# Separate tiles for the high and low parts of both layers' weights, one subtraction and a copied tail in the second layer, rotations that end in one sum

## The chip, the cores and the metric

The kernel runs on one core of a Trainium2 chip. The metric is the time of the whole program on the device in microseconds (us), lower being better. The engines are named as in the profile: PE (TensorE, matmuls), PEld (its weight loads), DVE (VectorE), ACT (ScalarE), POOL (GpSimd) and SP (SyncE). SP and POOL issue the transfers between the device memory and the chip's own memory (SBUF).

## The reference

One layer of a sequence model works on 2048 tokens of 576 numbers, in float32. A condition vector gives six modulation rows. The first half is a diagonal state-space convolution over the whole length, the second a feed-forward net with ReLU and 4608 hidden units:

```python
x = A_u                                            # 1 x 2048 x 576
mod = (_silu(c) @ w_mod).reshape(1, 6, 1, -1)      # sa, ca, ga, sb, cb, gb
h = _layernorm(x) * (1 + ca) + sa
# K[d, l] = 2 Re sum_n C[d, n] dt[d] exp(A[d, n] dt[d] l),  l = 0..2047
y = irfft(rfft(h, 4096) * rfft(K, 4096))[:2048] + h * D_skip
x = x + ga * y
h = _layernorm(x) * (1 + cb) + sb
x = x + gb * (relu(h @ w1) @ w2)                   # w1: 576 x 4608, w2: 4608 x 576
```

## The kernel before

**Stages.** The tokens are four blocks of 512. From the start to about 225 us the kernel computes the modulation, the powers from which the long filter K is built, and the convolution of block 0. Then the feed-forward net runs over the blocks 0 to 3, and beside it a generator of other work, a piece at a time: beside block 0 the rest of the filter (`rest`, with 12 "heads") and the convolution of block 1; beside block 1 the end of block 0, another six heads of `rest`, and the convolution of block 2; beside block 2 the end of block 1 and the convolution of block 3; beside block 3 the end of block 2.

**Two parts of each number.** TensorE multiplies in a reduced float32 format (`F32R`). To keep the accuracy, each factor is split into a high part (rounded to that format) and a low part (the rest), and a product takes three matmuls: high by high, high by low, low by high. The hidden layer is cut into 36 slices of 128 units, so that g runs from 0 to 143 over the four blocks. For each slice `first(g)` does 14 matmuls of 128x512 into the bank `hps`; ACT takes the ReLU's high part (`hh`, L1337) and DVE the low one (`hl`, L1338); `second(g-1)` does 14 more into the accumulators `acc`. On PE `first(g+1)` comes ahead of `second(g)`.

**The weights.** For each slice SP loads the raw weights of layer one (`r1`) and layer two (`r2`). ACT rounds them: `hi1` (L1297, 640 columns) and `hi2` (L1307, 576 columns). In block 0 DVE subtracts to get the low parts: `lo1` (L1302, 640 columns) and `lo2` (L1313 for the last 64 columns, L1314 for the first 512). SP then stores the low parts to device memory (`L1d`, `L2d`, L1415), and in the blocks 1 to 3 loads them back (L1286, L1317) so that DVE needn't compute them again. High and low part of a slice of layer one lie in one tile `w1`, of which there are three; those of layer two in one tile `w2` of 1152 columns, also three. A tile may be written again only when everything that read or wrote its old contents is done. So `hi1` waits, beside the matmuls, for the store of the old low part to have landed. In `w2` the last 64 high columns and the last 64 low ones lie side by side, because `second` multiplies them in one 128-column weight (into `acc4`).

**Rotations.** A head of `rest` turns complex numbers W by complex factors Z: it needs, per rotation, two multiplications of 128x1536 (T = W times the imaginary part, L482; W1r = W times the real part, L484) and two sums of 128x768 (real part minus, L486; imaginary part plus, L488). Block 0 has 24 rotations, block 1 has 12. W0 and Z (in the profile `Zr`) are loaded through POOL's queue; the load of a head's Z stands right behind that of its W0, which waits until a buffer of W0 is free. After the rotations PE forms the products `kps` in two halves (L517, 96 small matmuls each) that ACT copies out (`ker`, L527); there is one bank for them, so the second half waits until the first is copied out.

**What sets the order.** Within each engine the order is fixed before the run by a scheduler that goes by the program order, the dependences and costs of its own. The program order is set by `step(g)`, four times per slice: it draws pieces from the generator until the yielded costs (the numbers behind `yield`, in us of DVE) reach a target that grows with g, at most 2.7 per call.

Of the kernel before, what the change touches and what calls it, by code (L numbers as in the profile page):

```python
# [18 lines left out]
P = 128  # L19
# [30 lines left out]
class KGen:  # L50
# [403 lines left out]
    def rest(self, psum, plan):  # L454
# [5 lines left out]
        with ExitStack() as ctx:  # L460
# [15 lines left out]
            def rot(out, X, Z, i):  # L476
                T = pt.tile([P, 2, H, 16], F32, tag="T", name="T")
                zr, zi = (
                    Z[:, i, r].unsqueeze(1).unsqueeze(3).broadcast_to([P, 2, H, 16])
                    for r in range(2)  # L480
                )
# [4 lines left out]
                v(out[:, 0], out[:, 0], T[:, 1], op=ALU.subtract)  # L486
                yield 0.95
                v(out[:, 1], out[:, 1], T[:, 0], op=ALU.add)  # L488
# [83 lines left out]
class Body:  # L572
# [692 lines left out]
    def ffn(self, gens):  # L1265
# [17 lines left out]
        def low1(g):  # L1283
            w = w1[g] = ff.tile([P, 2, 5, P], F32R, tag="w1", bufs=3, name="w1")
            if g >= NF:
                nc.sync.dma_start(  # L1286
                    out=w[:, 1].rearrange("p k c -> p (k c)").bitcast(F32), in_=self.L1d[g % NF]
# [8 lines left out]
        def hi1(g):  # L1296
            copy(g - 1)(w1[g][:, 0], r1[g], AF.Copy)  # L1297

        def lo1(g):
            w, r = w1[g], r1.pop(g)  # L1300
            if g < NF:
                vec(g)(w[:, 1], r, w[:, 0], op=ALU.subtract)  # L1302
                late.append((self.L1d[g], w[:, 1].rearrange("p k c -> p (k c)")))

        def hi2(g):
            w = w2[g] = ff.tile([P, 1152], F32R, tag="w2", bufs=3, name="w2")
            copy(g)(w[:, 0:D], r2[g], AF.Copy)  # L1307

        def lo2(g):
            w, r = w2[g], r2.pop(g)  # L1310
            if g < NF:
                v = vec(g)
                v(w[:, D:640], r[:, 512:D], w[:, 512:D], op=ALU.subtract)  # L1313
                v(w[:, 640:], r[:, :512], w[:, :512], op=ALU.subtract)  # L1314
                late.append((self.L2d[g], w[:, D:]))
            else:
                nc.sync.dma_start(out=w[:, D:].bitcast(F32), in_=self.L2d[g % NF])  # L1317

        def first(g):
# [3 lines left out]
            ops = [(w[:, 0, 4], xs), (w[:, 1, 4], xs)]  # L1323
            if g:
                for k in range(4):
                    ops += [(w[:, 0, k], xh[:, k]), (w[:, 0, k], xl[:, k]), (w[:, 1, k], xh[:, k])]
# [237 lines left out]
```

## Time and profile before

| | |
|---|---|
| median of 3 runs | 1333.58 us (1330.17 to 1338.6) |
| the profiled execution | 1333.12 us, span 1331.4 us |
| mean granted clock of TensorE | 0.945 of full speed |
| PE busy | 1209.0 us, 91% |
| DVE busy | 895.4 us, 67% |
| ACT busy | 494.5 us, 37% |
| POOL busy | 162.8 us, 12% |

The page's times are those of one execution. Busy is the sum of an engine's instructions. The timeline prints for each instruction its start, its length, the engine, line, operation, output and inputs, and in brackets how long the engine stood idle before it and what ended that wait. The view by stretches of time prints per stretch its length, then for PE, PEld, DVE, ACT and POOL the busy time with the number of instructions, then the granted clock of TensorE, the share of the DMA engines and GB/s. The accumulators are copied out (L1443) at 549.73, 1091.73 and 1317.91 us for the blocks 0, 2 and 3, and the rotations run on DVE from 233 to 393 us (block 0) and from 572 to 643 us (block 1).

### The profile page before, as it was taken

To read this page: it belongs to the slowest core of one execution; us is meant where nothing else is said; L and a number is where in the kernel's file an instruction comes from. 1 tells how busy PE (TensorE), PEld (TensorE's weight loads), DVE (VectorE), ACT (ScalarE), POOL (GpSimd) and SP (SyncE) were. 2 spreads that over 40 slices of the span, in tenths; PEclk is the share of its full clock that TensorE was granted. 3 is DMA by queue.
4 is the path that set the end of the run, shared out by engine and by line. 5 is a ranking of instruction groups with operands and counts; after the bars stand their busy time and mean duration, and the time that the engine had idled before them with its cause. 6 is when DMAs were issued, how large, how long until landed. Compare 5 with 4: busy or idle time off the path is not lost.

```text
span 1331.4 us, 25993 instructions
## 1 busy us (share of the span) xinstructions
PE 1209.0 (91%) x10720; PEld 956.7 (72%) x10720; DVE 895.4 (67%) x1324; ACT 494.5 (37%) x863; POOL 162.8 (12%) x260
## 2 busy tenths in 40 slices
PE   4566676989989999999999999999999999999997
PEld 3344554667767687777777887887888888888885
DVE  5989988999986999689468993558995231111112
ACT  5678623222223422622243225433223453232321
POOL 0756502011000100100001000100000000000000
PEclk9557788999999999999999999999999999999999
DMA  8557982989878967799879985868996557666651
GB/s 272 214 221 296 304 307 84 350 296 331 307 253 304 337 224 277 247 402 342 281 276 338 357 321 156 288 203 305 346 363 198 175 181 223 198 198 202 192 168 54
DMA packets 122379, 345.85 MB, mean 260 GB/s; under 512 B 23916, under 2 KB 24212, under 8 KB 111508
## 3 DMA queue, kind: packets, MB, share of 16 engines
q1 hardware_dynamic: 105364, 226.96, 51.2%
q0 software_dynamic: 16384, 115.85, 23.1%
q8 instruction: 84, 1.38, 0.4%
q10 hardware_dynamic: 512, 1.38, 0.3%
q14 instruction: 35, 0.29, 0.1%
HBM read 262.73 MB, written 81.40 MB: 258 GB/s over the span
## 4 chain that ended last, share of the span: by engine, by line
PE 68%; DVE 17%; DMA 7%; issue 4%; ACT 2%; POOL 1%; SPq 0%; ACTq 0%; DVEq 0%; POOLq 0%
PE acc L1358 28%; PE hps L1332 27%; PE ps_f L852 5%; DMA L1d<-w 3%; PE kps L71 2%; PE ph L71 2%; DVE T L482 2%; DVE W1r L484 2%; PE ps_i L1059 2%; PE kps L517 1%; DVE w L1302 1%; DVE W1r L486 1%; DVE W1r L488 1%; DVE w L1314 1%; DVE T L62 1%
## 5 line engine op out<-in xcount | busy, mean ns | idle before, releaser
L1332 PE MATMUL hps<-xh,w 128*128 128x512 f32 x1152 | 395.2, 403 | 1.2 <-ACT xh L47 1.2
L1358 PE MATMUL acc<-w,hh 128*128 128x512 f32 x1152 | 366.4, 400 | 3.3 <-ACT hh L1337 3.2
L1338 DVE SCALAR_TENSOR_TENSOR hl<-hps,hh 128x512 fp32r<-128x512 f32 x144 | 99.0, 687 | 311.5 <-ACT hh L1337 310.8
L1332 PEld LDWEIGHTS hps<-xh,w 128*128 128x128 f32 x1152 | 217.8, 190 | 49.7 <-ACT xh L47 2.5
L1358 PEld LDWEIGHTS acc<-w,hh 128*128 128x128 f32 x1152 | 215.1, 188 | 50.6 <-ACT hh L1337 4.1
L1332 PE MATMUL hps<-xl,w 128*128 128x512 f32 x576 | 228.5, 397 | 0.7 <-DVE xl L47 0.5
L1358 PE MATMUL acc<-w,hl 128*128 128x512 f32 x576 | 223.1, 399 | 1.8 <-DVE hl L1338 1.8
L1337 ACT ACTIVATE hh<-hps 128x512 fp32r<-128x512 f32 x144 | 86.0, 597 | 327.7 <-PE hps L1332 320.5
L1307 ACT ACTIVATE w<-r 128x576 fp32r<-128x576 f32 x141 | 96.7, 686 | 216.5 <-PE acc L1358 216.1
L1332 PEld LDWEIGHTS hps<-xl,w 128*128 128x128 f32 x576 | 109.4, 190 | 24.7 <-DVE xl L47 1.7
L1358 PEld LDWEIGHTS acc<-w,hl 128*128 128x128 f32 x576 | 107.7, 189 | 26.1 <-DVE hl L1338 3.7
L1297 ACT ACTIVATE w<-r 128x640 fp32r<-128x640 f32 x140 | 102.6, 733 | 59.1 <-DMA L1d<-w 53.8
L1332 PE MATMUL hps<-xs,w 128*128 128x512 f32 x288 | 97.8, 409 | 0.0
L71 PE MATMUL kps<-W,W 128*32 128x16 f32 x2304 | 39.6, 210 | 47.3 <-POOL W L68 28.4
L1038 DVE TENSOR_TENSOR Y<-Y,T 128x1152 f32<-128x1152 f32 x60 | 79.3, 1349 | 0.0
L71 PEld LDWEIGHTS kps<-W,W 128*32 128x32 f32 x2304 | 34.8, 143 | 60.7 <-POOL W L68 31.0
L853 ACT ACTIVATE Z<-ps_f 128x288 f32<-128x288 f32 x120 | 49.0, 410 | 70.5 <-PE ps_f L852 68.5
L517 PEld LDWEIGHTS kps<-W1r,W2r 128*32 128x32 f32 x3456 | 45.2, 113 | 38.4 <-issue 19.7
L517 PE MATMUL kps<-W1r,W2r 128*32 128x48 f32 (+2 forms) x3456 | 52.5, 202 | 15.6 <-ACT ker L527 9.4
L1478 POOL DMA_DIRECT2D out_dram<-x x16 | 8.7, 545 | 466.9 <-DVE x L1470 464.5
L1332 PEld LDWEIGHTS hps<-xs,w 128*128 128x128 f32 x288 | 53.2, 188 | 11.1
L1358 PE MATMUL acc<-hh,w 128*128 128x512 f32 x144 | 57.5, 399 | 0.0
(235 smaller groups left out, 1574.5 us busy)
## 6 DMA issues: line engine op xcount, KB each, us to landing
r<-in_w_dram SPq DMA_DIRECT2D x144, 320.0 KB, 6.0
r<-in_w_dram SPq DMA_DIRECT2D x144, 288.0 KB, 3.9
w<-L1d SPq DMA_DIRECT2D x108, 320.0 KB, 4.1
w<-L2d SPq DMA_DIRECT2D x108, 288.0 KB, 2.8
W2r<-W2d POOLq DMA_DIRECT2D x18, 1536.0 KB, 9.4
W2d<-W SPq DMA_DIRECT2D x12, 1536.0 KB, 8.6
Ua<-Ud POOLq DMA_DIRECT2D x15, 1152.0 KB, 9.5
W<-W1d POOLq DMA_DIRECT2D x18, 768.0 KB, 9.6
```

The lines of the kernel that those rows point to most:

```text
L71: self.tc.keep_in_program_order(self.nc.tensor.matmul(*args, **kw))
L482: v(T, X, zi, op=ALU.mult)
L517: nc.tensor.matmul(ps[32 * dd : 32 * dd + 32, q, :], W2[:, r, ch], W1[:, r, ch], start=(r == 0), stop=(r == 1),)
L852: nc.tensor.matmul(o, fc[:, n2, c, :], src(n2), start=True, stop=True)
L853: ev = nc.scalar.activation(Z[:, n2, c], ps[:, :PC], AF.Copy)
L1038: v(y, y, T, op=op or ALU.add)
L1297: copy(g - 1)(w1[g][:, 0], r1[g], AF.Copy)
L1307: copy(g)(w[:, 0:D], r2[g], AF.Copy)
L1332: nc.tensor.matmul(ps, a, x, start=(i == 0), stop=(i == 13))
L1337: nc.scalar.activation(hh, ps, AF.Relu)
L1338: nc.vector.scalar_tensor_tensor(hl, ps, 0.0, hh, op0=ALU.max, op1=ALU.subtract)
L1358: nc.tensor.matmul(acc[i], a, x, start=(f == 0 and seen[i] == 1), stop=(f == NF - 1 and seen[i] == (3 if i < 4 else 2)),)
```

## The change

There are four edits.

1. Layer one: the high part lies in a tile `w1h` of its own (three of them), the low part in a tile `w1l` (four of them).
2. Layer two: the high part lies in `w2h` (640 columns, three tiles), the low part in `w2l` (576 columns, three tiles). `lo2` is one subtraction of 576 columns. The last 64 low columns must still lie beside the last 64 high ones, so ACT copies them: one new ACT instruction of 128x64 per slice (after.py L1317), in all 144 slices. In block 0 it reads what `lo2` wrote, in the blocks 1 to 3 what the load of `L2d` brought.
3. Rotations: Z has a third row, minus the imaginary part, which a new ACT instruction (L490, 128x2x48, one per head, 18 in all) makes from the loaded row; so it waits for the load. The load's rows are no longer contiguous in the tile. T then holds W times (imaginary, minus imaginary), and one sum of 128x1536 with T's halves swapped (L485) ends the rotation.
4. At a block's end the tile t4 is taken from a shared tile.

```diff
-                Z = pt.tile([P, 2, 2, H], F32, tag="Z", bufs=3, name=f"Zr_{h}")
+                Z = pt.tile([P, 2, 3, H], F32, tag="Z", bufs=3, name=f"Zr_{h}")
                 d(out=W0.rearrange("p r c a -> p (r c a)"), in_=k.W1d[h])
-                d(out=Z.rearrange("p i r c -> p (i r c)"), in_=k.Zd[h])
+                d(out=Z[:, :, 0:2], in_=k.Zd[h].rearrange("p (i r c) -> p i r c", i=2, r=2))
...
-                v(out[:, 0], out[:, 0], T[:, 1], op=ALU.subtract)
-                yield 0.95
-                v(out[:, 1], out[:, 1], T[:, 0], op=ALU.add)
-                yield 0.95
+                v(out, out, T[:, ::-1], op=ALU.add)
+                yield 1.75
 
             def rots(h, W1, W0, Z):
                 blocks = plan[h]
+                nc.scalar.activation(Z[:, :, 2], Z[:, :, 1], AF.Copy, scale=-1.0)
...
-            w = w1[g] = ff.tile([P, 2, 5, P], F32R, tag="w1", bufs=3, name="w1")
+            w = ff.tile([P, 5, P], F32R, tag="w1l", bufs=4, name="w1l")
+            w1[g] = [None, w]
...
-            copy(g - 1)(w1[g][:, 0], r1[g], AF.Copy)
+            w = w1[g][0] = ff.tile([P, 5, P], F32R, tag="w1h", bufs=3, name="w1h")
+            copy(g - 1)(w, r1[g], AF.Copy)
...
-            w = w2[g] = ff.tile([P, 1152], F32R, tag="w2", bufs=3, name="w2")
+            w = ff.tile([P, 640], F32R, tag="w2h", bufs=3, name="w2h")
+            w2[g] = w, ff.tile([P, D], F32R, tag="w2l", bufs=3, name="w2l")
             copy(g)(w[:, 0:D], r2[g], AF.Copy)
...
-                v = vec(g)
-                v(w[:, D:640], r[:, 512:D], w[:, 512:D], op=ALU.subtract)
-                v(w[:, 640:], r[:, :512], w[:, :512], op=ALU.subtract)
-                late.append((self.L2d[g], w[:, D:]))
+                vec(g)(l, r, w[:, 0:D], op=ALU.subtract)
+                late.append((self.L2d[g], l))
             else:
-                nc.sync.dma_start(out=w[:, D:].bitcast(F32), in_=self.L2d[g % NF])
+                nc.sync.dma_start(out=l.bitcast(F32), in_=self.L2d[g % NF])
+            copy(g)(w[:, D:], l[:, 512:], AF.Copy)
```

The order on the engines moves as follows. First ACT where the rotations of block 0 end. Before (w1 and w2 are the weight tiles, r1 and r2 the raw weights, hh the hidden slices 17 and 18, ker the copies out of the products):

```order
L1337 ACTIVATE hh_5214<-hps_5186 128x512
L1297 ACTIVATE w1_5224<-r1_5002 128x640
L527 ACTIVATE ker_6_3271<-kps_5066 128x16x6
L527 ACTIVATE ker_6_3271<-kps_5123 128x16x6
L1307 ACTIVATE w2_5302<-r2_5004 128x576
L1337 ACTIVATE hh_5298<-hps_5275 128x512
```

The slice 18's `hh` is the first row here, behind the two copies of the second-last head's products. The same place now:

```order
L1338 ACTIVATE hh_5130<-hps_5059 128x512
L525 ACTIVATE ker_0_3118<-kps_4917 128x48x6
L1317 ACTIVATE w2h_4954<-w2l_4955 128x64
L525 ACTIVATE ker_0_3118<-kps_4996 128x48x6
L1308 ACTIVATE w2h_5259<-r2_4899 128x576
L1317 ACTIVATE w2h_5134<-w2l_5135 128x64
L525 ACTIVATE ker_6_3281<-kps_5073 128x16x6
L525 ACTIVATE ker_6_3281<-kps_5143 128x16x6
L1317 ACTIVATE w2h_5259<-w2l_5260 128x64
L1297 ACTIVATE w1h_5358<-r1_5053 128x640
L1338 ACTIVATE hh_5255<-hps_5226 128x512
```

The first row is the slice 17's `hh`, the last the slice 18's; between them stand both heads' copies, one `hi2`, one `hi1` and three of the new tail copies (L1317).

Next ACT at the start of block 1's rotations, from the slice 38's `hh` to the slice 40's. Before:

```order
L1337 ACTIVATE hh_6572<-hps_6557 128x512
L1297 ACTIVATE w1_6580<-r1_6483 128x640
L1307 ACTIVATE w2_6619<-r2_6485 128x576
L1337 ACTIVATE hh_6615<-hps_6600 128x512
L1297 ACTIVATE w1_6623<-r1_6553 128x640
L1307 ACTIVATE w2_6674<-r2_6555 128x576
L1337 ACTIVATE hh_6670<-hps_6655 128x512
```

And now:

```order
L1338 ACTIVATE hh_6642<-hps_6627 128x512
L490 ACTIVATE Zr_6_6607<-Zr_6_6607 128x2x48
L1308 ACTIVATE w2h_6692<-r2_6552 128x576
L1317 ACTIVATE w2h_6692<-w2l_6693 128x64
L1297 ACTIVATE w1h_6755<-r1_6623 128x640
L1338 ACTIVATE hh_6688<-hps_6673 128x512
L490 ACTIVATE Zr_7_6613<-Zr_7_6613 128x2x48
L1308 ACTIVATE w2h_6750<-r2_6625 128x576
L490 ACTIVATE Zr_8_6715<-Zr_8_6715 128x2x48
L1317 ACTIVATE w2h_6750<-w2l_6751 128x64
L1297 ACTIVATE w1h_6810<-r1_6669 128x640
L1338 ACTIVATE hh_6746<-hps_6731 128x512
```

Three of the new negations (L490, the heads 6, 7 and 8) stand between the three `hh`, each ahead of the next slice's `hh`. The next one (head 9) stands behind the slice 41's `hh` and right ahead of the first `ker` of this block:

```order
L1338 ACTIVATE hh_6801<-hps_6786 128x512
L490 ACTIVATE Zr_9_6842<-Zr_9_6842 128x2x48
L525 ACTIVATE ker_6_6814<-kps_6815 128x32x6
L1308 ACTIVATE w2h_6911<-r2_6729 128x576
L1317 ACTIVATE w2h_6911<-w2l_6912 128x64
```

On ACT the copy of the products thus comes only after this head's load.

Last DVE, within a rotation of block 0 (T and W1r as above, hl the hidden slice's low part). Before:

```order
L1338 SCALAR_TENSOR_TENSOR hl_3731<-hps_3713,hh_3730 128x512
L486 TENSOR_TENSOR W1r_2_3600<-W1r_2_3600,T_3663 128x48x16
L488 TENSOR_TENSOR W1r_2_3600<-W1r_2_3600,T_3663 128x48x16
L1313 TENSOR_TENSOR w2_3734<-r2_3447,w2_3734 128x64
L482 TENSOR_TENSOR T_3721<-W1r_2_3600,Zr_2_3238 128x1536
```

And now:

```order
L485 TENSOR_TENSOR W1r_2_3611<-W1r_2_3611,T_3676 128x96x16
L1339 SCALAR_TENSOR_TENSOR hl_3744<-hps_3727,hh_3743 128x512
L481 TENSOR_TENSOR T_3719<-W1r_2_3611,Zr_2_3245 128x1536
L1313 TENSOR_TENSOR w2l_3748<-r2_3447,w2h_3747 128x576
L1302 TENSOR_TENSOR w1l_3675<-r1_3445,w1h_3752 128x640
```

One sum (L485) stands for the two, and one subtraction (L1313, now 576 columns) for L1313 and L1314.

More of the change, by code (lines that the diff above doesn't have):

```diff
@@ L477, in rot @@
                 T = pt.tile([P, 2, H, 16], F32, tag="T", name="T")
[L478 to L481, printed above, removed]
+                cb = [P, 2, H, 16]
+                zr = Z[:, i, 0].unsqueeze(1).unsqueeze(3).broadcast_to(cb)
+                zi = Z[:, i, 1:3].unsqueeze(3).broadcast_to(cb)
                 v(T, X, zi, op=ALU.mult)
@@ L1466, in finish @@
         yield None
-        t = self.cv.tile([P, 4, 64], F32, tag="t4", bufs=1, name="t4")
+        t = self.half("t4")[:, :, 0:64]
         v(t, ps, gb[:, 512:].unsqueeze(1).broadcast_to([P, 4, 64]), op=ALU.mult)
```

21 lines of the change are left out of this document (11 added, 10 removed).

## The prediction

> **What bounds the kernel now.** I read the page's head first, then the busy times by stretch, cut at the ends of the rotations, of two stalls and of the blocks.
>
> ```profile
> span 1331.4 us, 25993 instructions
> PE 1209.0 (91%) x10720; PEld 956.7 (72%) x10720; DVE 895.4 (67%) x1324; ACT 494.5 (37%) x863; POOL 162.8 (12%) x260
> 224.80:394.00 169.20, 153.65 (x2512) 117.82 (x2512) 164.20 (x176) 44.56 (x81) 18.52 (x35) 0.98 0.84 304
> 394.00:402.40 8.40, 7.44 (x117) 5.68 (x121) 0.11 (x2) 1.99 (x6) 1.05 (x1) 0.60 0.46 184
> 402.40:510.70 108.30, 108.01 (x638) 83.49 (x638) 95.36 (x155) 36.88 (x74) 8.25 (x15) 1.00 0.82 295
> 510.70:520.50 9.80, 6.80 (x23) 4.81 (x22) 9.16 (x12) 3.10 (x5) 0.00 (x0) 0.83 0.77 306
> 520.50:549.70 29.20, 29.12 (x130) 22.95 (x128) 23.09 (x53) 14.47 (x27) 0.00 (x0) 1.00 0.72 235
> 549.70:823.00 273.30, 271.76 (x2261) 215.24 (x2260) 208.37 (x265) 99.73 (x186) 24.89 (x43) 1.00 0.85 307
> 823.00:1091.70 268.70, 268.70 (x1181) 218.16 (x1180) 166.87 (x234) 99.12 (x178) 12.37 (x22) 1.00 0.75 257
> ```
>
> In the rotations of block 0 (to 394 us) DVE is full: 164.20 of 169.20. From 402 us PE is full, and stays so through the blocks 1 and 2 (271.76 of 273.30, 268.70 of 268.70). So the blocks 1 and 2 can only lose by a change that leaves PE's work alone, as this one does. Gains are to be had in block 0: on DVE in the rotations, and in the two short stretches with clocks 0.60 and 0.83. What ends the waits there shows in the list of waits and the timelines of ACT, PE and DVE:
>
> ```profile
> ACT w L1297 <- DMA L1d<-w: 53.8, 11, 11.3
> 393.29 0.74 ACT L1297 ACTIVATE w<-r 128x640 fp32r<-128x640 f32 x1 [6.99 <-DMA L1d<-w]
> 394.50 0.41 ACT L527 ACTIVATE ker<-kps 128x288 f32<-128x288 f32 x1
> 394.96 2.17 PE L517 MATMUL kps<-W1r,W2r 128*32 128x48 f32 x96 [4.70 <-ACT ker L527]
> 402.38 0.69 DVE L1338 SCALAR_TENSOR_TENSOR hl<-hps,hh 128x512 fp32r<-128x512 f32 x1 [8.29 <-ACT hh L1337]
> 513.96 0.74 ACT L1297 ACTIVATE w<-r 128x640 fp32r<-128x640 f32 x1 [11.34 <-DMA L1d<-w]
> 515.81 0.50 PE L1358 MATMUL acc<-w,hh 128*128 128x512 f32 x1 [2.77 <-ACT hh L1337]
> ```
>
> `hi1` waits eleven times, 53.8 us together, for the store of the old low part. At 393 and 514 us this reaches PE: `hi1` holds ACT, behind it stand `ker` or `hh`, and PE stops and then runs at a lower clock. The other nine lie under DVE's rotations.
>
> **Edit 1, `hi1` without the store.** With its own tile `hi1` waits only for matmuls that are done.
>
> First stall: PE stood from 390.26 (394.96 less 4.70), 3.74 us of it ahead of 394.00. Behind that 8.40 us passed with 7.44 busy at clock 0.60, which is 7.44 x 0.60 = 4.5 at full clock. At most 3.74 + 8.40 - 4.5 = 7.6 us come back. Not quite all: the last head's products need DVE's last rotation, which ends at the first stretch's end, and `hh` now stands behind both heads' copies and three tail copies. I take 6.5, and a range of 3 to 7.6.
>
> Second stall: 9.80 - 6.80 x 0.83 = 4.2 us at most. But DVE is busy for 9.16 of these 9.80, and the low parts that PE wants come from there; I take 2, range 0 to 4.2.
>
> The store's wait moves to `lo1` on DVE, where `w1l` has four tiles instead of three: one slice later. A slice is at least the 6.35 us from one `hh` to the next (580.28 to 586.62 below), so of 11.34 at most 5.0 would be left, and of 6.99 some 0.6.
>
> **Edits 2 and 3 on DVE.** What an instruction costs on a full engine is the distance between starts, not its length:
>
> ```profile
> 344.93 0.94 DVE L486 TENSOR_TENSOR W1r<-W1r,T 128x768 f32<-128x768 f32 x1
> 345.79 0.95 DVE L488 TENSOR_TENSOR W1r<-W1r,T 128x768 f32<-128x768 f32 x1
> 346.66 0.21 DVE L1313 TENSOR_TENSOR w<-r,w 128x64 fp32r<-128x64 f32 x1
> 346.80 1.75 DVE L482 TENSOR_TENSOR T<-W,Zr 128x1536 f32<-128x1536 f32 x1
> 348.47 0.68 DVE L1314 TENSOR_TENSOR w<-r,w 128x512 fp32r<-128x512 f32 x1
> 349.07 0.81 DVE L1302 TENSOR_TENSOR w<-r,w 128x640 fp32r<-128x640 f32 x1
> 436.16 0.75 DVE L867 TENSOR_TENSOR W<-Z 128x576 f32<-128x576 f32 x1
> 436.82 0.75 DVE L873 TENSOR_TENSOR K<-W 128x576 f32<-128x576 f32 x1
> 257.86 1.76 DVE L484 TENSOR_TENSOR W1r<-W,Zr 128x1536 f32<-128x1536 f32 x1 [1.88 <-PE kps L517]
> 314.47 1.76 DVE L484 TENSOR_TENSOR W1r<-W,Zr 128x1536 f32<-128x1536 f32 x1 [1.76 <-PE kps L517]
> ```
>
> Two sums: 346.66 - 344.93 = 1.73; one 1536-element instruction: 348.47 - 346.80 = 1.67. A rotation saves 0.06, 24 rotations 1.4 us. `lo2`: 0.14 + 0.60 (346.66 to 346.80, 348.47 to 349.07) against 0.66 for 576 elements (436.16 to 436.82): 0.08, and 1.4 over the 18 slices that the rotations span. Together 2.8. By plain lengths it would be 0.94 + 0.95 - 1.75 = 0.14 and 0.21 + 0.68 - 0.75 = 0.14, so 24 x 0.14 + 18 x 0.14 = 5.9; I go by the starts, since DVE is full, and keep 5.9 as the far end.
>
> [...]
>
> DVE also waits twice for `kps`, 1.88 + 1.76 = 3.6 us, where ACT's `ker` had stood behind a waiting `hi1`; I take half, 1.8. Against that stands edit 3's negation early on: ahead of the third slice's `hi1` ACT now waits for the third head's Z, and DVE's `lo1` behind it comes late. The bounds are 0 and a Z load's landing (below); I take 1.8. The remaining negations in block 0 stand ahead of `hh`s that DVE reaches microseconds later, so I cost them at nothing; without that cover each costs what Z is late. The rotations: -2.8 - 1.8 + 1.8 = -2.8.
>
> **Edit 3 in block 1.** Here PE is full, and the negation puts a DMA wait into ACT's queue: `hi2`, `hi1`, `hh` and `ker` queue behind it, and PE behind these. The rows of before, with POOL's issues of Z:
>
> ```profile
> 573.34 0.60 ACT L1337 ACTIVATE hh<-hps 128x512 fp32r<-128x512 f32 x1 [2.49 <-PE hps L1332]
> 580.28 0.60 ACT L1337 ACTIVATE hh<-hps 128x512 fp32r<-128x512 f32 x1 [2.49 <-PE hps L1332]
> 586.62 0.60 ACT L1337 ACTIVATE hh<-hps 128x512 fp32r<-128x512 f32 x1 [2.48 <-PE hps L1332]
> 588.18 0.39 PE L1358 MATMUL acc<-w,hl 128*128 128x512 f32 x1
> 595.07 0.72 PE L517 MATMUL kps<-W1r,W2r 128*32 128x32 f32 x48
> 571.60 1.76 DVE L482 TENSOR_TENSOR T<-W,Zr 128x1536 f32<-128x1536 f32 x1 [9.63 <-DMA Zr<-Zd]
> 576.44 0.55 POOL L47 DMA_DIRECT2D Zr<-Zd  x1
> 588.03 0.54 POOL L47 DMA_DIRECT2D Zr<-Zd  x1
> DMA to landing us min/median/max: 2.3/8.5/15.9
> L527 ACT ACTIVATE ker<-kps 128x192 f32<-128x192 f32 x12 | 4.0, 337 | 5.7 <-PE kps L517 5.7
> ```
>
> Head 6: Z lands by 571.6; negation 0.3 (an estimate from `ker`, 0.34), `hi2` 0.6, tail 0.2, `hi1` 0.65 bring `hh` of slice 39 to 573.3, where it is now: free. Head 8: issued at 576.44, landing 8.5 later at 584.9; then negation, tail and `hi1` bring `hh` of slice 40 (580.28) to 586.1, and `hl` to about 587.4. PE wants that `hl` at 588.18: free, barely. Head 9: issued at 588.03, landing at 596.5, and only then `ker` of the first products, at 596.9 to 597.2; PE wants to begin their second half at 595.07 now. It stops for 2.1 us, and about 1 more goes to the clock behind a stop, as at 394 and 511 us. The heads 10 and 11 stand where PE, by then 3 us later, leaves room. I take 3; with landings of 2.3 it is 0, with 15.9 it is 595.07 to 604.6, 9.5, and some 3 for the clock.
>
> **Edit 2's tail copies.** In block 0 the copy waits for `lo2`, and stands where DVE has done it. In the blocks 1 to 3 it waits for the load of `L2d`:
>
> ```profile
> w<-L2d SPq DMA_DIRECT2D x108, 288.0 KB, 2.8
> 438.01 0.69 ACT L1307 ACTIVATE w<-r 128x576 fp32r<-128x576 f32 x1
> 438.80 0.41 ACT L853 ACTIVATE Z<-ps_f 128x288 f32<-128x288 f32 x1
> 440.05 0.41 ACT L853 ACTIVATE Z<-ps_f 128x288 f32<-128x288 f32 x1 [0.84 <-PE ps_f L852]
> ```
>
> That load can issue when the low tile's last matmul is done, about 0.7 us before `hi2` can start, so 2.8 later it has landed 2.1 behind `hi2`'s start; in the plain slices ACT waits 2.5 us for `hh` anyway, so it is covered. In the convolutions of the blocks 1 and 2 one copy of a spectrum (Z) follows `hi2`, then the tail, and the next Z is due 1.25 us after the one before: 440.05 - 438.01 = 2.0 behind `hi2`. It comes some 0.3 us late, against 0.84 that it has. I take 1.5 for about eleven such tails, range 0 to 4. Edit 4 moves one small tile: nothing.
>
> **The sum**: -6.5 - 2 - 2.8 + 3 + 1.5 = -6.8 on 1333.12, so 1326.3 for an execution like the profiled one; the median of the runs stands 0.46 above that: 1326.8, say 1327.
>
> **The rivals.** *All of the slack comes back*: the stalls whole (7.6 + 4.2), both `kps` waits (3.6), the merges by plain lengths (5.9), and no Z late: -21.3, 1312. For it: of all heads' Zs DVE waited long for one, at 571.60. Against it: DVE's 9.16 of 9.80 in the second stall. 0.25.
>
> *The store's wait only moves*, to `lo1` on DVE, which in block 0 has no room, or `hh` loses behind tail copies that wait for `lo2` what `hi1` gains: then the first stall gives 3, the second nothing, the rotations nothing, and block 1 takes its 4.5: +1.5, 1335. For it: DVE's 164.20 of 169.20. Against it: the fourth tile. 0.20.
>
> *The negation holds ACT*, on the other side: Z landing near 15.9, as it did at its worst. It decides from the point where head 9's Z lands after 595: block 1 pays 12.5, the tails 4, and in block 0 four of the twelve heads let DVE wait 3 us each, 12, against gains of 6.5 + 2 + 2.8: +17.2, 1351. For it: W0's 768 KB go ahead of each Z in the same queue. Against it: the median of 8.5. 0.13. [...]
>
> **The numbers.** The forecast has 0.42, and by its own bounds reaches from 1318 to 1335. A difference of 1%, 13 us, is about what can be told apart from no change. Faster by more takes a time under 1320: the first rival and a little of the forecast, 0.28. Slower by more, over 1347: most of the third, 0.12. Within: 0.60. The range reaches into both outer rivals, 1312 to 1345.
>
> **What would show it.** In the profile of the changed kernel: no wait of `hi1` for `L1d`, and no stretch at a clock of 0.60 about 390 us; DVE's rotations ending near 390; block 0 ending near 538 instead of 549.70, the cut in the stretches; ACT's negations waiting for Zr, and a PE wait for `ker` of 2 us about 585; the blocks 1 and 2 together longer by 4 to 5 than their 273.30 + 268.70 = 542.0 us. I am wrong if `lo1` or the tail copies show the waits that `hi1` had, if DVE waits in the rotations for negations, or if block 1 loses more than 6 us.

## The result, and the profile after

| | us |
|---|---|
| before, median of 6 runs | 1332.29 (1328.69 to 1338.60) |
| after, median of 6 runs | 1390.21 (1388.14 to 1398.36) |
| ratio after to before, 95% interval | 1.0443 (1.0412 to 1.0475) |
| profiled execution of after | 1390.04, span 1388.3 |

The changed kernel is 58 us slower. That is outside the range, and beyond even the rival on the slow side (1351). The head of its page, and the two groups of ACT and DVE that changed most:

```profile
span 1388.3 us, 26053 instructions
PE 1226.9 (88%) x10720; PEld 969.9 (70%) x10720; DVE 891.3 (64%) x1252; ACT 524.3 (38%) x1025; POOL 165.9 (12%) x260
L1339 DVE SCALAR_TENSOR_TENSOR hl<-hps,hh 128x512 fp32r<-128x512 f32 x144 | 99.4, 691 | 370.2 <-ACT hh L1338 370.0
L1317 ACT ACTIVATE w2h<-w2l 128x64 fp32r<-128x64 f32 x141 | 35.9, 254 | 274.2 <-DMA w2l<-L2d 267.0
```

ACT's new copy of the tail (line 1317) is 35.9 us of work in an engine that is idle for 62% of the span; but ACT stood still for 267.0 us ahead of it, waiting for the load of the second layer's low part.

Where the time went shows in the busy times by block, cut at the copies of `acc` out of PSUM that end each block. The columns are the stretch, its length, the busy times of PE, PEld, DVE, ACT and POOL, the granted clock, the DMA share and GB/s. First after:

```profile
224.80:553.80 329.00, 306.17 (x3423) 238.88 (x3422) 288.62 (x334) 111.86 (x244) 30.09 (x50) 0.96 0.81 290
553.80:872.90 319.10, 291.20 (x2296) 227.92 (x2295) 208.44 (x253) 107.16 (x230) 26.02 (x43) 0.97 0.77 268
872.90:1150.20 277.30, 263.29 (x1132) 212.06 (x1132) 165.24 (x231) 101.62 (x208) 12.34 (x22) 0.97 0.72 241
1150.20:1376.30 226.10, 226.10 (x1003) 187.43 (x1002) 30.57 (x46) 75.71 (x141) 2.17 (x4) 1.00 0.61 181
```

and the same cuts in the kernel before:

```profile
224.80:549.70 324.90, 305.02 (x3409) 234.75 (x3409) 291.92 (x393) 101.00 (x190) 27.83 (x50) 0.97 0.81 292
549.70:833.80 284.10, 282.56 (x2309) 224.15 (x2308) 210.08 (x267) 103.66 (x193) 24.89 (x43) 1.00 0.84 303
833.80:1091.70 257.90, 257.90 (x1133) 209.25 (x1132) 165.16 (x231) 95.19 (x172) 12.37 (x22) 1.00 0.76 259
1091.70:1317.90 226.20, 226.20 (x1003) 187.45 (x1002) 30.46 (x46) 67.60 (x108) 2.18 (x4) 1.00 0.61 182
```

Block 0 is 4 us longer where 11 were to be gained, block 1 is 35.0 longer, block 2 19.4 longer, and block 3 the same. (From block 1 some twelve matmuls have moved to block 0, as the counts show; what moves them is said with the table of the experiments.) In block 1 PE, which had no room, now stands idle for 319.1 - 291.2 = 27.9 us, and its granted clock is 0.97 where it was 1.00.

Block 3 has the tail copies too, 34 of them in this cut. ACT's waits for the load, in the lists of waits cut to the blocks 1 and 3 (us in total, times, longest):

```profile
ACT w2h L1317 <- DMA w2l<-L2d: 126.6, 31, 12.2
ACT w2h L1317 <- DMA w2l<-L2d: 53.2, 34, 3.0
```

In block 3 ACT waits 53.2 us and nothing is lost; in block 1 it waits 126.6. What differs is how long the load takes to land. It is the same 288 KB through the same queue; its median is the last number in these rows, from the DMA views of after, cut to the blocks 1, 2 and 3:

```profile
w2l<-L2d SPq DMA_DIRECT2D x36, 288.0 KB, 5.1
w2l<-L2d SPq DMA_DIRECT2D x36, 288.0 KB, 3.2
w2l<-L2d SPq DMA_DIRECT2D x34, 288.0 KB, 2.8
```

The medians alone don't tell the loss apart, since that of block 2 is close to that of block 3. The longest landings are 8.9, 7.4 and 4.3 us, and ACT's timeline has 20 waits of more than 2.5 us for the load in block 1, 11 in block 2 and one in block 3. What they have above 2.5 us adds up to 59.1, 25.4 and 0.5 us.

How a late load reaches PE is seen in one place in block 1, where the convolutions run. The timelines of SP's queue, ACT and PE of after:

```profile
738.38 0.33 SPq L1316 DMA_DIRECT2D w2l<-L2d  x1
...
739.08 0.69 ACT L1308 ACTIVATE w2h<-r 128x576 fp32r<-128x576 f32 x1 [1.21 <-PE acc L1359]
739.67 0.39 ACT L851 ACTIVATE Z<-ps_f 128x288 f32<-128x288 f32 x1
740.90 0.41 ACT L851 ACTIVATE Z<-ps_f 128x288 f32<-128x288 f32 x1 [0.84 <-PE ps_f L850]
746.37 0.26 ACT L1317 ACTIVATE w2h<-w2l 128x64 fp32r<-128x64 f32 x1 [5.05 <-DMA w2l<-L2d]
746.53 0.39 ACT L851 ACTIVATE Z<-ps_f 128x288 f32<-128x288 f32 x1
...
741.63 0.65 PE L850 MATMUL ps_f<-kt,fcK 128*128 128x288 f32 x2
742.34 0.39 PE L1333 MATMUL hps<-xh,w1h 128*128 128x512 f32 x1
...
746.98 1.33 PE L850 MATMUL ps_f<-kt,fcK 128*128 128x288 f32 x2 [4.01 <-ACT Z L851]
747.69 1.04 PE L1333 MATMUL hps<-xh,w1l 128*128 128x512 f32 x1
```

The load is issued at 738.38 and its copy starts 8.0 us later. The matmuls of the next spectrum, issued at 741.63, had taken 0.65 us, but its copy (`Z`, line 851) stands behind the tail on ACT and starts at 746.53, 0.16 us after the tail does. PE stops for 4.01 us until `Z` is copied. Behind the stop two matmuls of 288 columns take 1.33 us and one of 512 takes 1.04, where ahead of it they had taken 0.65 and 0.39. Two loads of 1152 KB each for the next convolution were issued meanwhile, at 739.30 and 739.82, and took 9.4 and 12.0 us.

### The profile page after: what moved, and what is told of

It is laid out like the page before. It is cut to its first block, busy times and chain, and to the rows that moved or that the text cites. A ratio compares the mean times of both kernels' runs of the same rounds, so it can differ in the third digit from the quotient of the medians.

```text
span 1388.3 us, 26053 instructions
## 1 busy us (share of the span) xinstructions
PE 1226.9 (88%) x10720; PEld 969.9 (70%) x10720; DVE 891.3 (64%) x1252; ACT 524.3 (38%) x1025; POOL 165.9 (12%) x260
## 4 chain that ended last, share of the span: by engine, by line
PE 61%; DVE 16%; DMA 13%; issue 6%; ACT 3%; POOL 1%; SPq 0%; ACTq 0%; POOLq 0%; DVEq 0%
PE acc L1359 24%; PE hps L1333 23%; DMA w2l<-L2d 7%; PE ps_f L850 4%; DMA Zr<-Zd 2%; PE kps L71 2%; PE ph L71 2%; PE ps_i L1057 2%; PE kps L515 2%; DVE T L1034 1%; DVE Y L1036 1%; DVE T L481 1%; DMA W<-W1d 1%; DVE W1r L485 1%; DVE W1r L483 1%
## 5 line engine op out<-in xcount | busy, mean ns | idle before, releaser
L1359 PE MATMUL acc<-w2h,hh 128*128 128x512 f32 x576 | 231.1, 406 | 9.7 <-ACT hh L1338 9.7
L1333 PE MATMUL hps<-xh,w1l 128*128 128x512 f32 x576 | 235.2, 408 | 0.0
L1333 PE MATMUL hps<-xh,w1h 128*128 128x512 f32 x576 | 233.7, 406 | 0.7 <-ACT xh L47 0.7
L1359 PE MATMUL acc<-w2l,hh 128*128 128x512 f32 x576 | 233.3, 410 | 0.0
L1333 PE MATMUL hps<-xl,w1h 128*128 128x512 f32 x576 | 229.1, 398 | 0.1
L1359 PE MATMUL acc<-w2h,hl 128*128 128x512 f32 x576 | 222.9, 400 | 2.5 <-DVE hl L1339 2.4
L1317 ACT ACTIVATE w2h<-w2l 128x64 fp32r<-128x64 f32 x141 | 35.9, 254 | 274.2 <-DMA w2l<-L2d 267.0
L1359 PEld LDWEIGHTS acc<-w2h,hh 128*128 128x128 f32 x576 | 110.6, 192 | 36.1 <-ACT hh L1338 12.3
L1333 PEld LDWEIGHTS hps<-xh,w1h 128*128 128x128 f32 x576 | 111.0, 193 | 25.3 <-ACT xh L47 1.3
L1333 PEld LDWEIGHTS hps<-xh,w1l 128*128 128x128 f32 x576 | 110.7, 192 | 24.1 <-issue 0.3
L1333 PEld LDWEIGHTS hps<-xl,w1h 128*128 128x128 f32 x576 | 110.3, 191 | 24.6 <-DVE xl L47 0.4
```

Source lines behind the costliest of these rows:

```text
L1317: copy(g)(w[:, D:], l[:, 512:], AF.Copy)
L1333: nc.tensor.matmul(ps, a, x, start=(i == 0), stop=(i == 13))
L1359: nc.tensor.matmul(acc[i], a, x, start=(f == 0 and seen[i] == 1), stop=(f == NF - 1 and seen[i] == (3 if i < 4 else 2)),)
```

## The experiments

Two theories stood first. **The tail theory**: the copy's wait for the load in ACT's queue is the loss, all of it, and edits 1 and 3 play no part in it. Against it, first, **the rival of the prediction**: the negation's wait for `Zr` in the same queue. Then, when edit 2 was seen to hold the loss, **a loop theory**: a late ACT frees raw tiles late, SP's raw loads then issue late, which makes ACT later still, so that the copy's own wait would be a small part. The block lengths below are the distances between the copies of `acc` (the first copy at each block's end) in each profile; those of block 3 agree to 0.6 us. The start of block 0, its first `hl`, lies between 228.74 and 234.68 us in the profiles, so block 0 is judged by the medians of the runs. One thing besides the waits changes the lengths: with edit 3 the pieces have other costs behind `yield`, and 9 to 21 matmuls of block 1 stand in block 0 instead (block 1 of before has 2309, that of edit 3 alone 2288). So the lengths of block 1 compare best among kernels that have edit 3, or among those that don't.

| kernel | block 1 | block 2 | block 3 | ratio to before (95%) |
|---|---|---|---|---|
| before | 284.0 | 258.0 | 226.2 | |
| after | 319.1 | 277.6 | 225.8 | 1.0443 (1.0412 to 1.0475) |
| after without edit 2 | 285.9 | 258.2 | 225.8 | 1.0084 (1.0047 to 1.0120) |
| edit 2 alone | 318.9 | 280.1 | 226.2 | 1.0432 (1.0386 to 1.0478) |
| after, tail by a load | 286.9 | 258.3 | 225.8 | 1.0032 (1.0015 to 1.0049) |
| after, load one slice earlier | 288.8 | 259.9 | 225.8 | 1.0102 (1.0061 to 1.0144) |
| after, tail copied behind `hh` | 289.1 | 257.9 | 225.6 | 1.0062 (1.0035 to 1.0088) |
| after, four raw tiles | 319.8 | 278.8 | 225.8 | 1.0434 (1.0383 to 1.0484) |

**After without edit 2, and edit 2 alone.** The second layer's tiles and subtractions as before, the rest as after; and the reverse.

```diff
-            w = ff.tile([P, 640], F32R, tag="w2h", bufs=3, name="w2h")
-            w2[g] = w, ff.tile([P, D], F32R, tag="w2l", bufs=3, name="w2l")
+            w = w2[g] = ff.tile([P, 1152], F32R, tag="w2", bufs=3, name="w2")
...
-            copy(g)(w[:, D:], l[:, 512:], AF.Copy)
```

> The changed kernel with edit 2 undone: layer two's parts lie in one tile again, DVE subtracts in two pieces, ACT copies no tail. Theory T (ACT's tail copy waits for the load of the stored low part, 267 us in 99 waits, and hi1, hh and the raw loads queue behind it): the time falls from 1390 to 1325-1340, the blocks 1 and 2 return to about 545 us together from some 581. Rival N (the negation holds ACT for the rotation factors): it stays at 1375-1390, since the negations are all still there. Rival O (hi1 now stands ahead of hh in ACT's order): 1360 or more if that order stays.

> The kernel before with edit 2 alone. Theory T: 1370-1395, ACT's tail copy waiting 200 us or more for the load. Rival N: within 5 us of before, 1330, since there are no negations.

Measured: 1343.99 us without it, 4 us above the theory's range, and 1390.20 with it alone. Edit 2 is the loss. The other edits together cost 0.8%, a matter apart that is followed up below. Where PE waits in block 1 with edit 2 alone, its list of waits tells:

```profile
PE kps L517 <- ACT ker L527: 9.2, 4, 5.8
PE ps_f L852 <- ACT Z L853: 8.6, 2, 5.2
```

Before, PE waited 1.3 us for `ker` in this block and not for `Z`.

**The tail by its own load.** In the blocks 1 to 3 the 64 tail columns come straight from DRAM into `w2h`, by a second, small load, and ACT copies nothing there. All else is as in after.

```diff
-                nc.sync.dma_start(out=l.bitcast(F32), in_=self.L2d[g % NF])
+                nc.sync.dma_start(out=l[:, 0:512].bitcast(F32), in_=self.L2d[g % NF][:, 0:512])
+                nc.sync.dma_start(out=w[:, D:].bitcast(F32), in_=self.L2d[g % NF][:, 512:])
+                return
             copy(g)(w[:, D:], l[:, 512:], AF.Copy)
```

> The changed kernel, but in the blocks 1 to 3 the 64 tail columns come by a load of their own (128 x 256 bytes) straight into the high tile, and the other 512 low columns by another; ACT copies the tail in block 0 only. Everything else is as in the changed kernel, and the bytes loaded are the same. Theory T: ACT waits for no load, 1325-1345. Rival C (the transfers themselves are slower, and whoever needs the low part is late): PE waits for them instead and the time stays above 1375.

Measured: 1335.91 us. The DMA view of this kernel, cut to block 1:

```profile
w2l<-L2d SPq DMA_DIRECT2D x36, 256.0 KB, 6.3
w2h<-L2d SPq DMA_DIRECT2D x36, 32.0 KB, 7.4
```

The loads land no sooner (6.3 and 7.4 us against 5.1), and block 1 takes 286.9 us where it took 319.1: no engine's list of waits has them any more, since PE wants them later than ACT did. So it isn't the load's lateness that costs, but that ACT waited for it.

**The load one slice earlier.** Four `w2l` tiles (and three `w1l`), and the load issued at the slice before.

```diff
+        def low2(g):
+            l = l2[g] = ff.tile([P, D], F32R, tag="w2l", bufs=4, name="w2l")
+            if g >= NF:
+                nc.sync.dma_start(out=l.bitcast(F32), in_=self.L2d[g % NF])
...
+                if g + 2 < n:
+                    low2(g + 2)
```

> The changed kernel, but the low part of layer two has four tiles (that of layer one three, for room) and its load is asked for one slice earlier; ACT's tail copies stay. Theory T with a loop (tail copy, hi1, raw load, next low load in SP's queue): a slice of 6.35 us more covers landings of 3 to 9 us nearly always, 1330-1350, tail waits under 60 us. Rival O (the copies' place in ACT's order, whatever they wait for): 1375 or more.

Measured: 1346.29 us, and the wait for the load is down from 267.0 us to this:

```profile
ACT w2h L1324 <- DMA w2l<-L2d: 38.3, 14, 6.4
```

The copy stays on ACT and costs little once its data are there. Some 14 us more than before are left, of which the kernel with the tail's own load has 4; this run alone doesn't divide the rest between the 14 waits that remain and the third `w1l` tile.

**The tail copied behind `hh`, and four raw tiles.** The first leaves the copy on ACT and its load where it is, but places it one slice later, behind `hh`. The second tests the loop theory: `r1` gets four tiles and `w1l` three, so that SP can issue the raw load a slice ahead of ACT.

```diff
-            copy(g)(w[:, D:], l[:, 512:], AF.Copy)
+            if g < NF:
+                copy(g)(w[:, D:], l[:, 512:], AF.Copy)
...
+            if g >= NF:
+                tw, tl = w2[g]
+                act(tw[:, D:], tl[:, 512:], AF.Copy)
             return hh, hl
```

```diff
-            w = ff.tile([P, 5, P], F32R, tag="w1l", bufs=4, name="w1l")
+            w = ff.tile([P, 5, P], F32R, tag="w1l", bufs=3, name="w1l")
...
-            r1[g] = ff.tile([P, 5, P], F32, tag="r1", bufs=3, name="r1")
+            r1[g] = ff.tile([P, 5, P], F32, tag="r1", bufs=4, name="r1")
```

> The changed kernel, but in the blocks 1 to 3 ACT copies a slice's tail behind that slice's hh instead of ahead of the hh before it: the same copies, the same loads at the same places of SP's queue, each copy one slice later. Theory T (a copy that waits for a load which lands within a slice holds what stands behind it): 1333-1345, tail waits under 30 us. Rival O (ACT has too many instructions, or the copies delay PE's second layer by themselves): above 1370.

> The changed kernel with four raw tiles of layer one instead of three (and three tiles w1l instead of four, for room): SP's next raw load, which stands ahead of the next load of the low part, no longer waits for the hi1 that stands behind ACT's tail copy. Theory L (the wait feeds itself: tail copy, hi1, raw load, low load, next tail copy): the loop is open, the tail waits fall to half or less, 1340-1365. Theory T without a loop (each landing is late by itself): 1380-1395 as with the change.

Measured: 1339.09 us behind `hh`, where ACT waits for `w2l` three times, 5.7 us together, and 1388.59 us with four raw tiles. The list of waits of the latter:

```profile
ACT w2h L1317 <- DMA w2l<-L2d: 259.4, 98, 12.4
```

So the loop theory falls: the waits and the time are close to those of after. The tail theory stands for nearly all of the loss: edit 2 undone, the tail loaded, the load earlier and the copy later each take away the waits or most of them, and all but 0.3 to 1.0% of the loss in time, and the fourth raw tile takes away neither.

**Edit 2 alone, its tail mended in both ways**: the kernel before with edit 2, and on that the diff of the tail's own load, or that of the copy behind `hh`.

> The kernel before with edit 2, but in the blocks 1 to 3 the tail columns come by a load of their own instead of ACT's copy. If the tail's wait is all that is bad in edit 2: block 0 ends at 547 as with edit 2 alone, the blocks 1 to 3 are as before, 1328-1331, the fastest so far. If the additional small loads cost: 1334 or more.

> The kernel before with edit 2 alone, ACT's tail copy placed one slice later in the blocks 1 to 3. Theory T: block 0 gains the 2.5 us that edit 2 alone showed, the rest is as before: 1328-1332, against 1390 for edit 2 alone. If the copies cost in the convolutions: 1335 or more.

Measured: with the tail by a load 1332.87 us, a ratio of 1.0007 (0.9986 to 1.0029): edit 2 without ACT's wait neither costs nor gains anything that can be told. With the copy behind `hh` it came out at 1341.44, 1.0074 (1.0045 to 1.0103), where the theory had no change, and in the range that was set for copies that cost in the convolutions. Its block 1 is 292.9 us, against 283.5 with the load, and PE waits there seven times for `Z`, 3.5 us together, where it doesn't with the load. This variant also fixes the order of `hh` and the copies; whether the copies themselves or that order make the waits is not shown.

**Edit 1 alone, and with edit 2 mended** (its tail by a load). These ask why block 0 gained nothing.

```diff
-            w = w1[g] = ff.tile([P, 2, 5, P], F32R, tag="w1", bufs=3, name="w1")
+            w = ff.tile([P, 5, P], F32R, tag="w1l", bufs=4, name="w1l")
+            w1[g] = [None, w]
...
+            w = w1[g][0] = ff.tile([P, 5, P], F32R, tag="w1h", bufs=3, name="w1h")
+            copy(g - 1)(w, r1[g], AF.Copy)
```

> The kernel before with edit 1 alone (layer one's parts in separate tiles). The prediction's step (the two stalls behind hi1's wait for the store come back): block 0 ends at 541 instead of 549.7 and the time falls by 8 to 1324. Rival O (hi1 now stands ahead of hh in ACT's order and waits there for matmuls or for its raw weights, so hh comes 0.65 us or more late where DVE is full): block 0 ends at 550-556, 1332-1340.

> The changed kernel without edit 3, and with the tail columns loaded in the blocks 1 to 3. Beside the run with all edits and the loaded tail (1336) the difference is edit 3 alone. The prediction's step (edit 3 costs block 1 some 3 us and gives block 0 nothing): 1331-1334. Rival O (edit 1 costs block 0): 1335 or more.

Measured: 1336.18 us, 1.0027 (1.0004 to 1.0051), and 1335.55 us, 1.0038 (1.0013 to 1.0064): no gain, rather a small loss. `hi1`'s waits for the store are gone, as the edit says. The list of waits of edit 1 alone (its profile is of its slowest execution, 1341.09 us) has another in their place, and the timelines of ACT and PE show it at the place of the second stall and a gap at that of the first:

```profile
ACT w1h L1299 <- DMA r<-in_w_dram: 41.7, 9, 10.2
511.79 0.74 ACT L1299 ACTIVATE w1h<-r 128x640 fp32r<-128x640 f32 x1 [10.20 <-DMA r<-in_w_dram]
516.19 0.69 ACT L1309 ACTIVATE w<-r 128x576 fp32r<-128x576 f32 x1 [3.17 <-DMA L2d<-w]
397.80 0.46 PE L517 MATMUL kps<-W1r,W2r 128*32 128x48 f32 x23
401.49 0.38 PE L517 MATMUL kps<-W1r,W2r 128*32 128x48 f32 x10 [3.23 <-issue]
```

`hi1` now waits 41.7 us for the raw weights, where it had waited 53.8 for the store. At 512 us it waits 10.20 us for the raw load, where it had waited 11.34 for the store at 514; and `hi2` after it waits for the store of the second layer's low part. At 401 PE stops inside a run of small matmuls for nothing that the profile shows ("issue"). Such stops stand ahead of the products' matmuls all through block 0. PE's lists of waits there, the first two rows of before, the others of edit 1 alone:

```profile
PE kps L517 <- ACT ker L527: 8.1, 3, 4.7
PE kps L517 <- issue: 5.7, 5, 2.0
...
PE kps L517 <- issue: 12.5, 6, 3.2
PE kps L517 <- ACT ker L527: 0.5, 1, 0.5
```

The waits for `ker` go from 8.1 to 0.5 us, and those that have no name go from 5.7 to 12.5. So PE stands about as long at the products as it did.

**Edit 1 with four raw tiles** (and three `w1l`), by itself and with edit 2's tail by a load; and the fourth raw tile in the kernel before, without any edit of the change.

```diff
-            r1[g] = ff.tile([P, 5, P], F32, tag="r1", bufs=3, name="r1")
+            r1[g] = ff.tile([P, 5, P], F32, tag="r1", bufs=4, name="r1")
```

> The kernel before with edit 1 but with three tiles w1l and four raw tiles r1. Edit 1 alone gave 1.0027 of before, with hi1 waiting 41.7 us for raw weights where it had waited 53.8 us for the store. Theory R (the raw load, which could start only when a raw tile was free, took the store's place): those waits fall under 20 us, block 0 ends near 545 and the time at 1325-1330. Rival D (the transfers are late as such, because block 0's DMA queues are full): the waits stay above 30 us, 1333-1338.

> The kernel before with edit 1 (three tiles w1l, four raw tiles) and edit 2 (tail columns loaded in the blocks 1 to 3), without edit 3. Edit 1 with four raw tiles gave 1.0009 and edit 2 with the loaded tail 1.0007. If each removes a wait that the other leaves standing: 0.994-0.998. If block 0 is held by its transfers: 0.999-1.004.

> The kernel before with four raw tiles of layer one instead of three, and nothing else: the control for the runs with four. If the fourth raw tile by itself makes the gain: 0.992-0.997 of before. If hi1's wait for the store hides it: within 0.998-1.003.

Measured: 1333.42 us, 1.0009 (0.9982 to 1.0035); 1329.43 us, 0.9978 (0.9956 to 0.9999); and the fourth tile on the kernel before, by itself, 1331.21 us, 0.9990 (0.9963 to 1.0018). Only the second, with both edits, is faster than before, by 0.2% and barely beyond the noise. The raw waits of the first are 8.2 us where edit 1 alone had 41.7:

```profile
ACT w1h L1299 <- DMA r<-in_w_dram: 8.2, 2, 6.0
```

Most of the second wait is gone too, and the time still doesn't move: at 508 us `hi2` waits 4.03 us for its store, at 514 `hi1` 5.96 for the raw load, and PE's stops without a name are 14.1 us in block 0, that at 397 being 2.93. So the waits fell as theory R had it, and the time is in rival D's range.

The control tells more than its time. With the fourth raw tile alone, `hi1`'s wait for the store falls from 53.8 us to this:

```profile
ACT w L1297 <- DMA L1d<-w: 17.7, 7, 6.1
```

So the store's wait didn't hide a gain of the fourth tile: 36 us less of ACT's waiting gave none that can be told.

**Edit 3 alone, its negation on DVE, and without any.**

```diff
-                nc.scalar.activation(Z[:, :, 2], Z[:, :, 1], AF.Copy, scale=-1.0)
+                nc.vector.tensor_scalar(Z[:, :, 2], Z[:, :, 1], -1.0, None, op0=ALU.mult)
```

```diff
-                nc.scalar.activation(Z[:, :, 2], Z[:, :, 1], AF.Copy, scale=-1.0)
...
-                zi = Z[:, i, 1:3].unsqueeze(3).broadcast_to(cb)
+                zi = Z[:, i, 1].unsqueeze(1).unsqueeze(3).broadcast_to(cb)
```

> The kernel before with edit 3 alone (third row of Z by a negation on ACT, one sum per rotation). The prediction's step: rotations of block 0 shorter by 1.4, less some 2 for early negations, block 1 longer by 3: 1332-1338. Rival N (negations cost block 0 most: ACT held for Z while hi1, hh and ker wait): block 0 ends at 555 or later, 1338-1345.

> The kernel before with edit 3 alone, the negation of the third row on DVE instead of ACT. Edit 3 alone on ACT gave 1.0059 of before. Rival N (ACT's negation, which holds hi1, hh and ker until Z lands, is what costs): 1328-1334, since DVE needs Z at that place anyhow. Rival M (the merged sum and the other pace of the pieces cost): 1338-1342 still.

> The kernel before with edit 3 alone and no negation at all: the imaginary part stands in both halves of T, so the sign of the real part's term is left out of the computation; each rotation is still two products and one sum. Rival N: 1327-1332, block 0 ending 1 to 3 us ahead of before. Rival M: 1338-1342.

Measured: 1340.23 us, 1.0059 (1.0036 to 1.0082), with the negation on ACT; 1333.33 us, 1.0007 (0.9989 to 1.0025), with it on DVE; 1333.13 us, 0.9998 (0.9984 to 1.0012), without. The list of ACT's waits of the first, and its timelines of ACT and PE at head 9:

```profile
ACT Zr L490 <- DMA Zr<-Zd: 34.7, 9, 10.1
600.04 0.28 ACT L490 ACTIVATE Zr<-Zr 128x96 f32<-128x96 f32 x1 [10.06 <-DMA Zr<-Zd]
600.23 0.32 ACT L525 ACTIVATE ker<-kps 128x192 f32<-128x192 f32 x1
600.61 1.49 PE L515 MATMUL kps<-W1r,W2r 128*32 128x32 f32 x96 [3.76 <-ACT ker L525]
```

So the negation's wait in ACT's queue is worth 0.5 to 0.6%, 7 to 8 us, and the merged sum nothing that can be told. Of the 34.7 us of waiting 24.8 lie in block 1 and 9.9 in block 0. DVE, which needs Z next in any case, does the same negation without loss.

**ACT's new waits for loads taken away.** All edits of the change, with the tail by its load and the negation on DVE; then the same with the fourth raw tile as well.

> The changed kernel with only its two ACT waits mended: tail columns loaded in the blocks 1 to 3 (that alone gave 1.0032 of before), and the negation on DVE; tiles as in the change (four w1l, three raw). If the negation on ACT costs here what it cost edit 3 alone (0.5%): 0.996-0.999. If the fourth raw tile is needed for any gain: 1.000-1.004.

> All the edits with each wait mended: four raw tiles, the tail columns loaded in the blocks 1 to 3, the negation on DVE. If ACT's waits were all that the change cost: 1322-1330, below before, with block 0 ending near 545. If the merges and tiles gain nothing in themselves: 1332-1338.

Measured: 1328.51 us, 0.9971 (0.9946 to 0.9997), and 1322.82 us (1319.06 to 1325.54), 0.9923 (0.9902 to 0.9944). The latter beats both kernels, by 10 us and by 67; all four of its executions are faster than the fastest of before beside them (1326.90). Its blocks 0 and 1 in the view by stretch, from its fastest execution:

```profile
224.80:542.20 317.40, 299.47 (x3424) 233.38 (x3422) 288.75 (x346) 109.40 (x230) 30.19 (x50) 0.98 0.84 300
542.20:821.30 279.10, 278.27 (x2291) 221.58 (x2290) 207.59 (x258) 100.94 (x187) 26.11 (x43) 1.00 0.86 306
```

Block 0 ends 7.5 us earlier than before, of which 2.4 are from its start (the first `hl` at 228.74 against 231.10), and block 1 takes 279.1 where it took 284.0. The last isn't a gain of block 1 by itself, as 18 of its matmuls have moved to block 0 (2291 against 2309). Both blocks together, from the first `hl`, take 592.5 us where they took 602.7. The parts don't add up to this: edit 2 mended 1.0007, edit 1 with the fourth tile 1.0009, edit 3 on DVE 1.0007. Each of them leaves ACT with other waits: 28.7 us for layer one's store with edit 2 mended, 41.8 with edit 3 on DVE, 16.2 for the second layer's store and the raw weights with edit 1. That this is why they give nothing one by one is argued and not shown.

## Why the prediction was wrong

**The step that failed: the tail copies**, "I take 1.5 ..., range 0 to 4". With edit 2 alone the blocks 1 and 2 are 34.9 + 22.1 = 57.0 us longer, and edit 2 alone is as slow as the whole change (1.0432 against 1.0443). The mechanism was named, a DMA wait that stands in ACT's queue ahead of a spectrum's copy and of `hh`, and so was the cover, 2.5 us of waiting for `hh`. What was wrong is the price of the wait: every copy got one landing of 2.8 us, a median of the page. The DMA view of the kernel before, cut to block 1 and (last row) to block 3, tells where it came from:

```profile
w<-L2d SPq DMA_DIRECT2D x36, 288.0 KB
r<-in_w_dram SPq DMA_DIRECT2D x36, 288.0 KB, 8.3
...
w<-L2d SPq DMA_DIRECT2D x34, 288.0 KB, 2.8
```

In block 1 of before the view has no landing at all for that load, and none in block 2: the 2.8 is block 3's alone, where the DMA share is 0.61 against 0.84. The page gave one figure for 108 loads that came from 34 of them at most. The row beside it was the nearer one: 288 KB through the same queue in the same block landed in 8.3 us. With 8.3 the prediction's own working gives 8.3 - 0.7 = 7.6 us behind `hi2`'s start, against a cover of 2.5; with the 5.1 that was then measured it is 4.4. So the wait was not covered.

But no median gives the size. In block 2 of after the median is 3.2, by which the working has 3.2 - 0.7 = 2.5, just covered, and block 2 still lost 19.4 us. What goes with the loss is the late landings: the 20 and 11 waits of ACT beyond 2.5 us, whose excess is 59.1 and 25.4 us in blocks that lost 35.0 and 19.4, while block 3, with one such wait, lost nothing. The bound of 4 us had been worked out for eleven tails in the convolutions; the slices beside the rotations were called covered, and lost too, as the 9.2 us that PE waits for `ker` with edit 2 alone show. Where 2.8 does hold, in block 3, the cover held as foretold.

**The first stall (-6.5) and the second (-2)** came to nothing: edit 1 alone is 1.0027. The store's wait went from `hi1`, as the prediction said, and didn't go to `lo1`, as the rival feared (in after DVE's `lo1` waits three times for `w1h`, 3.7 us together). It went to the raw load behind it, 41.7 of 53.8 us, and in after block 0 has 20.1 us of it, the longest 7.83 at 392 us, the very place of the first stall. I had asked whether the wait would come back on DVE, and hadn't asked what else `hi1` needs: its raw load, which reuses a tile that the late subtraction frees. The rival "the store's wait only moves" was right in kind, wrong in place. With the fourth raw tile that wait is mostly gone too, and edit 1 still gains nothing: at the first stall PE then stops in the last products without a wait that the profile names, and why is open.

**The rotations (-2.8)**: the merges' share was -1.4 for edit 3's 24, and the starts bear it out. In block 0 of before the next instruction starts 0.87 us behind each of the two sums, and in after 1.67 behind the merged one, so a merge saves DVE 0.07 us, and 24 save 1.7. Plain lengths had 24 x 0.14 = 3.4 us, twice what the starts give. In the time nothing shows: without the negation the ratio is 0.9998 (0.9984 to 1.0012), which is -2.1 to +1.6 us. (The page's busy time counts overlapping instructions once, and is not their sum: the lengths of before's DVE instructions, mean times count by form, add up to 979 us, and its busy time is 895.4.) The rotations end at 394.03 + 1.76 = 395.8 us in after, not near 390; in the last kernel, at 384.5. DVE's waits for `kps` in the rotations, of which half was to go, are 7.8 us in after where they were 3.6.

**The negations.** Edit 3 alone loses 7.9 us, where the working has 1.8 + 3 - 1.4 = 3.4. With the negation on DVE, and the same pieces in each block, block 1 takes 280.3 us and with it on ACT 283.3, so the +3 for block 1 came out right. That was partly luck. Head 9's negation starts at 600.04 where 596.5 was taken, and PE, which works on until 596.85, stops for 3.76 us where 2.1 was taken; and the row at 595.07 isn't where the second half begins in before. The halves have 96 matmuls each:

```profile
586.51 1.17 PE L517 MATMUL kps<-W1r,W2r 128*32 128x32 f32 x96
587.74 0.33 ACT L527 ACTIVATE ker<-kps 128x192 f32<-128x192 f32 x1
591.00 0.72 PE L517 MATMUL kps<-W1r,W2r 128*32 128x32 f32 x48
595.07 0.72 PE L517 MATMUL kps<-W1r,W2r 128*32 128x32 f32 x48
```

The second half begins at 591.00, 4 us earlier than the working had it. Block 0 from its first `hl` is 0.8 us longer with the negation on ACT (324.5 against 323.7), so some 3 of the 6.9 us between the two kernels' runs aren't found in the profiles. The rival had the mechanism, and its 12 us for block 0 didn't come. Z's loads of 96 KB, with their rows no longer contiguous, landed with medians of 9.1 us in after, 8.6 in edit 3 alone and 7.9 with the negation on DVE, against 8.5 before, so by 0.6 us later at most. Whether the rows' layout has a part in that, these medians don't settle.

**The chances.** The 0.12 for slower was all given to one of the two edits that put a new DMA wait into ACT's queue, the negation, and the other had no rival of its own.

What stays open: PE's stops without a named wait in the products of the rotations; why the copy behind `hh` costs edit 2 alone 0.7%; where some 3 of the 7 us of the negation's loss lie; and how the last kernel's 10 us divide among its edits.

## What to carry to other kernels

On ACT here, an instruction that waited for a DMA held up what stood behind it, though it was short and the engine idle for 62% of the span of after: 72 copies of 0.25 us in two blocks made them 57 us longer, and the same data by a second load cost nothing that can be told (1.0007). It did little or no harm where the data came in time (the load a slice earlier, 38.3 us of waiting in 14 waits; block 3, 53.2 us with none over 3.0) or where the engine needed the data next anyhow (the negation on DVE, 1.0007). Price a load by its landings in the stretch where it will be waited for, the late ones as well as the median, and look first whether the page's median comes from that stretch at all; where the view gives none there, take the nearest transfer of that stretch that has one. And when a wait is removed, list everything else that its instruction needs, since the gain can end at the next of these.

## What the runs showed of the hardware

In after the same load of 288 KB through the same queue landed in 2.7 to 4.3 us in block 3 (DMA share 0.61), and in 2.9 to 8.9 in block 1 (0.77) with transfers of 1152 KB from POOL's queue beside it. Nor did a small load land sooner there: with the tail by a load, the 32 KB tail, issued behind the 256 KB of the same slice (a median of 6.3 us in block 1), took a median of 7.4 us in block 1 and 2.2 in block 3. That the large transfers cause it goes with these numbers, and no run took them away.

In both kernels and in ten of the variants PE stops in the small matmuls of the products with no wait that the profile names: five times and 5.7 us together in before, six times and 9.5 us in after, seven times and 14.1 us with edit 1 and the fourth raw tile. Some stand at the same place of the program with other lengths: ahead of the last 13 matmuls of 128x16 of a run, 1.72 us in before, 3.13 with the fourth raw tile alone, 3.24 with edit 1 alone and 4.47 with both. No run here tells why.
